# A two-part kernel (local and pooled attention, then a spatially gated MLP): mask and pooled v on TensorE for the first six head pairs, one buffer stock, and another table of durations for the planner

## The chip, the core and the metric

The kernel runs on one core of a Trainium2 chip. The metric is the device time of one execution in microseconds (us). The core has five engines with queues of their own, each worked off strictly in order: TensorE (PE in the profile, PEld for its weight loads), VectorE (DVE), ScalarE (ACT), GpSimdE (POOL) and SyncE (SP), which here only issues DMAs. The engines wait for each other by semaphores.

## The reference

Inputs are q, k, v of shape (8 batches, 8 heads, 576 positions, 64), all float32. For each head there are two attentions, and their sum is the head's output:

```python
q_d, k_d, v_d = means of q, k, v over groups of 4 positions      # 144 positions
out_up    = repeat(softmax(q_d k_d^T / 8) v_d, 4)                # pooled attention
out_local = softmax(where(|i - j| < 4, q k^T / 8, -1e9)) v       # a band of 7 keys per row
x = heads side by side of (out_up + out_local)                   # (8, 576, 512)

h = gelu_tanh(x @ w_in)                    # w_in 512 x 1024
u, v = two halves of h
v_n = (v - mean) / sqrt(var + 1e-6) * g_ln
v_s = w_sg @ v_n + b_sg                    # w_sg 576 x 576, over positions
out = x + (u * v_s) @ w_out                # w_out 512 x 512
```

## The kernel before, in words

The work of a batch has two parts. **Attention** goes by pairs of heads, four pairs (128 partitions: two heads of 64) per batch, 32 in all, numbered g. **The MLP** follows per batch and needs all four pairs of its batch.

Local attention is done in 10 blocks of 58 queries against 64 keys. For a pair the steps are (names of the tasks in the code in brackets): loads of q, k, and v in two layouts (lq, lk, lv, lw); sums of four neighbours of q, k and v (qs, ks, vs), the q sums spread by DMA into a block-diagonal tile (qx); the score product (S, line L403, 40 rows on TensorE); the mask of 0 and -1e30 added by VectorE while it copies the scores from PSUM to the tile ms, in two halves (ma, mb, L410); row maxima (mx, L424) and their product with minus the scale, the bias of the exponential (L426); exponentials with row sums on ScalarE (ea, eb, L436); reciprocals (rc); normalisation (np, L454). Pooled attention has the same steps on a smaller tile: Y (L420), my (L430, L431), ec (L444), nq (L457). The weights are then transposed by TensorE (T, U, t: L462, L467 and L469, L475), copied from PSUM (pa, pb, pc, pe), and multiplied with v: d (L500, pooled) and D (L520, local). VectorE adds both (xa, xb, L527), and x is split into a high and a low part (xh, xl, xc), so that three products of the faster float type give a float32 product.

The MLP has the products v (5 parts, L601), u, s and o (8 parts each, L680), with gelu, layer norm (vb, vp, vn: L632, L643, L651), splits (vh, vl, gh, gl: L198, L671, L735), bias and gate (sa, sm) and the final addition and store (oa, os) between. The last split ahead of the o product is gl (L735). At the start the weights are read as pairs of 32-bit words of a 64-bit format and turned into high and low parts: 24 pieces (eight each named y, z and r) through wb (L266, L268), wu, wq, wf (L282), wt (L287), wh (L198), wl (L293); w_sg needs whq and wlq alone.

The order is set by a planner that runs when the kernel is built. Every step is a `Task` with the engines that can do it and a duration on each, the tasks it comes after, the buffers it takes and gives back, and perhaps a due time. `plan` walks through a time of its own, gives a free engine the ready task with the least latest start, and so fixes, for each engine, the order in which its instructions are written. The chip then keeps that order and nothing else of the plan. `SIZES` and `CAPS` say how many buffers there are and how many of them a kind may hold: `ps` are the eight PSUM banks, `X`, `R` and `x` tiles in SBUF.

## Time and profile before

| | |
|---|---|
| runs | 664.25, 664.43, 661.49 us; median 664.25 us |
| the profiled execution | 664.12 us, of which the span from first to last instruction is 662.3 us |
| mean granted TensorE clock | 0.951 |
| busy: PE, PEld, DVE, ACT, POOL | 91%, 82%, 76%, 52%, 38% of the span |
| instructions | 16062 |
| chain that ended last | PE 72%, DVE 20%, issue 2%, POOL 2%, ACT 2%, DMA 1% |
| DMA | 60.29 MB, 91 GB/s on average |

How to read it: a busy share is a mean over the whole span, and the stages differ. The windows view gives busy time by stretch, the timeline the single instructions with the idle time before them and who ended it, the groups the mean duration by line and shape. PE rows are pipelined and their ends are modelled, so neighbouring rows overlap. An fp32 matmul shows as two rows.

### The profile page before, as it was taken

The numbers are of one execution on the slowest core, as the hardware profiler recorded it, in microseconds if no ns is written. First come the engines' busy times: TensorE is split into PE (matmuls) and PEld (weight loads), VectorE is DVE, ScalarE is ACT, GpSimd is POOL, SyncE is SP. The second block draws the span as 40 slices with busy tenths as digits, with TensorE's granted clock in tenths as the row PEclk, the third lists the DMA queues.
The fourth block names the chain that finished last, engine by engine and source line by source line (L and its number), as shares of the span: only waits on it lengthen the run. The fifth ranks groups of instructions, "written<-read, shape, count | busy, mean of one in ns | idle before, by whom it ended". The sixth has DMA issues, their size and how long they took to land.

```text
span 662.3 us, 16062 instructions
## 1 busy us (share of the span) xinstructions
PE 602.1 (91%) x6240; PEld 545.2 (82%) x6240; DVE 502.8 (76%) x1017; ACT 347.0 (52%) x1226; POOL 253.3 (38%) x298
## 2 busy tenths in 40 slices
PE   3767783989999999999999999999999999989997
PEld 3656572988899988989799888988898978979997
DVE  4899999999867949794888849794879759644452
ACT  3775776854757436654664446463664446350300
POOL 3476355474223424242434333342434233211210
PEclk9976766998999999999999999999999999989999
DMA  7666423423222330334222331224133430001001
GB/s 212 213 179 183 123 87 105 121 79 114 92 81 79 116 111 14 94 94 132 63 80 81 115 112 51 75 77 137 57 82 82 130 98 21 2 19 54 1 1 72
DMA packets 72684, 60.29 MB, mean 91 GB/s; under 512 B 17312, under 2 KB 56480, under 8 KB 72608
## 3 DMA queue, kind: packets, MB, share of 16 engines
q1 hardware_dynamic: 72608, 59.27, 29.8%
q8 instruction: 49, 0.80, 0.5%
q14 instruction: 27, 0.22, 0.1%
HBM read 47.45 MB, written 9.44 MB: 86 GB/s over the span
## 4 chain that ended last, share of the span: by engine, by line
PE 72%; DVE 20%; issue 2%; POOL 2%; ACT 2%; DMA 1%; SPq 0%; DVEq 0%; POOLq 0%; ACTq 0%
PE ps L680 43%; PE ps L601 14%; PE ps L520 3%; PE ps L403 3%; PE ps L500 3%; PE ps L420 3%; DVE ms L454 2%; PE ps L462 2%; DVE R L268 2%; DVE R L282 1%; DVE R L735 1%; ACT ms L436 1%; DVE stats L424 1%; DVE vs L716 1%; DVE ms L410 1%
## 5 line engine op out<-in xcount | busy, mean ns | idle before, releaser
L680 PE MATMUL ps<-wsg_h,R 128*128 128x288 f32 x576 | 123.0, 300 | 0.0
L680 PE MATMUL ps<-R,wout_h 128*128 128x288 f32 x512 | 111.3, 303 | 2.0 <-ACT wout_h L198 1.2
L436 ACT ACTIVATE ms<-ms,nb 128x64 f32<-128x64 f32 x320 | 106.8, 337 | 8.8 <-DVE nb L426 8.5
L680 PEld LDWEIGHTS ps<-wsg_h,R 128*128 128x128 f32 x576 | 93.7, 189 | 2.2 <-issue 1.2
L680 PE MATMUL ps<-wsg_l,R 128*128 128x288 f32 x320 | 92.5, 295 | 0.0
L680 PEld LDWEIGHTS ps<-R,wout_h 128*128 128x128 f32 x512 | 85.0, 191 | 4.3 <-ACT wout_h L198 1.4
L680 PE MATMUL ps<-X,win_h 128*128 128x288 f32 x256 | 80.3, 314 | 5.4 <-ACT R L697 2.9
L680 PE MATMUL ps<-R,win_h 128*128 128x288 f32 x256 | 77.8, 304 | 0.0
L680 PE MATMUL ps<-X,win_l 128*128 128x288 f32 x256 | 77.6, 303 | 0.0
L680 PE MATMUL ps<-R,wout_l 128*128 128x288 f32 x256 | 76.2, 298 | 0.3 <-DVE wout_l L293 0.3
L457 POOL TENSOR_TENSOR pd<-pd,rc 96x432 f32<-96x432 f32 x30 | 38.9, 1297 | 94.3 <-DVE rc L451 92.9
L601 PE MATMUL ps<-win_h,X 128*128 128x512 f32 x160 | 66.9, 418 | 1.4 <-ACT win_h L198 1.4
L601 PE MATMUL ps<-win_l,X 128*128 128x512 f32 x160 | 64.6, 404 | 3.8 <-DVE win_l L293 3.8
L751 DVE TENSOR_TENSOR x<-ps,x 128x288 f32<-128x288 f32 x64 | 29.0, 453 | 42.3 <-PE ps L680 42.3
L436 ACT ACTIVATION_READ_ACCUMULATOR ms<-ms,nb 128x1 f32 x320 | 60.7, 190 | 0.0
L680 PEld LDWEIGHTS ps<-wsg_l,R 128*128 128x128 f32 x320 | 60.3, 188 | 0.0
L680 PEld LDWEIGHTS ps<-X,win_h 128*128 128x128 f32 x256 | 50.4, 197 | 7.4 <-ACT R L697 3.3
L716 DVE SCALAR_TENSOR_TENSOR vs<-ps,g_sb,b_sb 128x288 f32<-128x288 f32 x64 | 32.8, 513 | 28.9 <-PE ps L680 28.7
L436 ACT ACT_TABLE_LOAD x22 | 28.2, 1283 | 48.6 <-DVE nb L426 48.4
L601 PE MATMUL ps<-win_h,R 128*128 128x512 f32 x128 | 51.4, 402 | 0.0
L680 PEld LDWEIGHTS ps<-R,win_h 128*128 128x128 f32 x256 | 50.5, 197 | 0.3
L680 PEld LDWEIGHTS ps<-X,win_l 128*128 128x128 f32 x256 | 50.4, 197 | 0.0
(103 smaller groups left out, 1385.9 us busy)
## 6 DMA issues: line engine op xcount, KB each, us to landing
vw<-in_vp_dram SPq DMA_DIRECT2D x64, 160.0 KB
q<-in_qT_dram SPq DMA_DIRECT2D x32, 293.0 KB
k<-in_kT_dram SPq DMA_DIRECT2D x32, 293.0 KB
v<-in_vp_dram SPq DMA_DIRECT2D x64, 144.0 KB
out_dram<-x SPq DMA_DIRECT2D x32, 288.0 KB
R<-in_w_in_dram SPq DMA_DIRECT2D x16, 256.0 KB
qd_bd<-qd SPq DMA_DIRECT2D x64, 36.0 KB
R<-in_w_out_dram SPq DMA_DIRECT2D x8, 256.0 KB
```

Source lines behind the costliest of these rows:

```text
L268: nc.vector.scalar_tensor_tensor(out=bits.bitcast(I32), in0=hw.bitcast(I32), scalar=-0x40000000, in1=bits.bitcast(I32), op0=ALU.bitwise_an ...
L403: nc.tensor.matmul(out=sp[i][os, c * KB:(c + 1) * KB], lhsT=q[hs, t * QB:t * QB + KB], rhs=k[hs, t * QB:t * QB + KB], start=True, stop=True)
L420: nc.tensor.matmul(out=st["sdv"][:, i, :], lhsT=qd_bd[par][:, i, :], rhs=st["kd"], start=True, stop=True)
L436: nc.scalar.activation(out=st["ms"][:, t, :], in_=st["ms"][:, t, :], func=AF.Exp, bias=st["nb"][:, t:t + 1], scale=scale, accum_out=sums[p ...
L454: ENG[e].tensor_tensor(out=st["ms"], in0=st["ms"], in1=bc_last(st["rc"][:, 0:NT], KB), op=ALU.mult)
L457: ENG[e].tensor_tensor(out=st["pd"], in0=st["pd"], in1=bc_last(st["rc"][0:96, NT:], SD), op=ALU.mult)
L500: nc.tensor.matmul(out=dn[hs].rearrange("p (i m) -> p i m", i=3), lhsT=vd[:, kt, hs], rhs=pdt[:, kt, :, h * 48:(h + 1) * 48], start=(kt == ...
L520: nc.tensor.matmul(out=at["ps", "o", g, i][hs, c * QB:(c + 1) * QB], lhsT=vw[ks, c, hs], rhs=pt[ks, c, h ^ i], start=True, stop=True)
L601: nc.tensor.matmul(out=acc, lhsT=r32(l), rhs=r32(w[:, k, DM:DF]), start=(i == 0), stop=(i == len(ops) - 1))
L680: nc.tensor.matmul(out=acc[:, 0:HALF], lhsT=r32(l), rhs=r32(r), start=(n == 0), stop=(n == len(ops) - 1))
L716: nc.vector.scalar_tensor_tensor(out=vsb[i], in0=at["ps", "m", b, "s", i][:, 0:HALF], scalar=g_sb[:, i // 2:i // 2 + 1], in1=b_sb[:, half( ...
L751: nc.vector.tensor_tensor(out=x[:, half(i)], in0=at["ps", "m", b, "o", i][:, 0:HALF], in1=x[:, half(i)], op=ALU.add)
```

## The change

For the first six pairs (`early`, g below 6: the four of batch 0 and two of batch 1):

- The mask is added on TensorE. Each of the two PSUM tiles of scores first gets a product of the identity with the mask (128 x 320), and the score products accumulate onto it. VectorE's two mask additions are gone; the row maxima read PSUM in two halves, and the exponentials read PSUM and write ms.
- The pooled product takes its four rows of v one by one: 16 small matmuls instead of 4, and GpSimdE's sum of v (vs, L391 and L392) is gone.

For all pairs the bias is a task of its own (nx, ny), which ScalarE or VectorE can do by a one-input multiplication. The loads of the first two pairs may be issued from ScalarE's queue. Attention tiles (q, k, the layouts of v, ms, pd, pt, pdt, x) come from the same stock of buffers as the MLP's, now 10 and 40; four PSUM banks instead of two may hold scores, two instead of one pooled scores. The planner has other durations, lengthens a VectorE task when GpSimdE works beside it and a TensorE task after idle time, holds loads back by a time given, and has other due times. So the order is another one throughout.

```diff
+COLD = 0.8
+AHEAD = 25.0
+SHARED = dict(np=0.6, nq=0.6, xl=0.6, wb=0.8, wf=0.6, wt=0.6, wl=0.6, wh=1.0, vn=0.3, vh=1.0, vl=0.6,
+              xh=1.0, sm=0.6, gh=1.0, gl=0.6, nx=0.3, ny=0.3)
+LONE = ("vp", "xc")
...
-    ready = [0.0] * n
+    ready = [max(t.hold, latest[i] - AHEAD) if t.mb else t.hold for i, t in enumerate(tasks)]
...
         end = now + t.engines[e]
+        if e == "V" and t.kind in SHARED:
+            end += SHARED[t.kind] * max(0.0, min(end, beside) - now)
+        if e == "P" and t.kind not in LONE:
+            beside = end
+        if e == "T":
+            idle = 0.85 * idle + 0.15 * min(1.0, (now - engine_at[e]) / 2.0)
+            end += COLD * min(1.0, 3.0 * idle) * t.engines[e]
...
-PERIOD, BASE, LEAD, MSBUFS = 67.0, 44.0, 12.0, 2
-SIZES = {"ps": 8, "X": 6, "R": 21, "x": 8}
-WIDTH = {"ps": 512, "X": XW, "R": S, "x": QB * NT}
-CAPS = {("ps", "s"): 2, ("ps", "d"): 1, ("ps", "t"): 3, ("ps", "o"): 2, ("ps", "m"): 4, ("R", "w"): 8, ("R", "v"): 3}
+PERIOD, BASE, LEAD, EARLY = 70.0, 40.7, 12.4, 6
+W_DUE = dict(y=40.0, z=53.0, r=84.0)
+HOLD = 0.0
+W_HOLD = dict(y=0.0, z=0.0, r=62.0)
+SIZES = {"ps": 8, "X": 10, "R": 40}
+WIDTH = {"ps": 512, "X": XW, "R": QPAD}
+CAPS = {("ps", "s"): 4, ("ps", "d"): 2, ("ps", "t"): 3, ("ps", "o"): 3, ("ps", "m"): 4, ("R", "w"): 12, ("R", "v"): 3,
+        ("R", "q"): 4, ("R", "k"): 4, ("X", "ms"): 4, ("X", "vw"): 4, ("R", "v4"): 8, ("R", "x"): 8}
...
         def scores(e):
             sp = [buf("ps", "s", g, i) for i in range(2)]
+            if early:
+                for i in range(2):
+                    nc.tensor.matmul(out=sp[i][:, 0:NTP * KB], lhsT=ident_sb, rhs=mask_sb[:, i:i + NTP, :],
+                                     start=True, stop=False, skip_group_check=True)
...
-                                         rhs=k[hs, t * QB:t * QB + KB], start=True, stop=True)
+                                         rhs=k[hs, t * QB:t * QB + KB], start=not early, stop=True,
+                                         skip_group_check=early)
...
         def top(e):
-            nc.vector.tensor_reduce(out=stats[par][:, 0:NT], in_=st["ms"], axis=AX.X, op=ALU.max)
-            st["nb"] = att.tile([P, NT + 3], F32, name="nb")
-            nc.vector.tensor_tensor(out=st["nb"][:, 0:NT], in0=stats[par][:, 0:NT], in1=nscale[:, 0:NT], op=ALU.mult)
+            if early:
+                for i in range(2):
+                    nc.vector.tensor_reduce(out=stats[par][:, i * NTP:(i + 1) * NTP], in_=spv(i), axis=AX.X, op=ALU.max)
+            else:
+                nc.vector.tensor_reduce(out=stats[par][:, 0:NT], in_=st["ms"].rearrange("p (c i) k -> p i c k", i=2),
+                                        axis=AX.X, op=ALU.max)
+
+        def bias(e):
+            st["nb"] = att.tile([P, NT], F32, name="nb")
+            if e == "A":
+                nc.scalar.mul(out=st["nb"], in_=stats[par][:, 0:NT], mul=-scale)
+            else:
+                nc.vector.tensor_scalar(out=st["nb"], in0=stats[par][:, 0:NT], scalar1=-scale, scalar2=None, op0=ALU.mult)
...
         def av_d(e):
-            for kt in range(2):
+            parts = [(kt, f) for kt in range(2) for f in range(FAC if early else 1)]
+            for n, (kt, f) in enumerate(parts):
                 for h in range(2):
...
+                                     lhsT=st["v4"][kt][:, f, hs] if early else st["vd"][:, kt, hs],
...
-        add(N("np"), {"P": 1.4, "V": 0.7}, norm, [N("rc")])
-        add(N("nq"), {"P": 0.96, "V": 0.5}, norm_d, [N("rc")])
+        add(N("np"), {"P": 1.42, "V": 0.78}, norm, [N("rc")])
+        add(N("nq"), {"P": 0.98, "V": 0.5}, norm_d, [N("rc")])
```

The order changes at every place; three of them follow. In these rows a line is one instruction or several equal ones (x), as out<-in with the program's names and the shape written. The first is the head of VectorE's queue, the first pair's steps. Before:

```order
L367 TENSOR_REDUCE qd<-q 128x144
L367 TENSOR_REDUCE kd<-k 128x144
L410 TENSOR_TENSOR ms<-ps_118,mask_sb 128x5x64
L410 TENSOR_TENSOR ms<-ps_119,mask_sb 128x5x64
L424 TENSOR_REDUCE stats_85<-ms 128x10
L426 TENSOR_TENSOR nb<-stats_85,nscale 128x10
```

And now, where lines have moved (L386 is L367 of before, L453 is L424, L463 the bias on VectorE), and where R_100 to R_108 are q and k of the first two pairs:

```order
L386 TENSOR_REDUCE qd<-R_100 128x144
L386 TENSOR_REDUCE kd<-R_102 128x144
L386 TENSOR_REDUCE qd<-R_105 128x144
L386 TENSOR_REDUCE kd<-R_108 128x144
L453 TENSOR_REDUCE stats_85<-ps_140 128x5
L453 TENSOR_REDUCE stats_85<-ps_141 128x5
L463 TENSOR_SCALAR nb<-stats_85 128x10
```

The second pair's sums have come ahead, and the mask additions are gone. The second place is TensorE's queue in batch 3 at the first transposes of that batch's time, those of the second pair of batch 4. Before, they stand after the second part of the u product:

```order
L680 MATMUL ps_4416<-R_4118,win_h 128x288
L680 MATMUL ps_4416<-X_4116,win_l 128x288
L475 MATMUL ps_4439<-ident_sb,pd 72x96 x3
L462 MATMUL ps_4445<-ident_sb,ms 128x128 x4
L467 MATMUL ps_4451<-ident_sb,ms 128x128
L469 MATMUL ps_4451<-ident_sb,pd 72x96 x3
```

Now they stand after its fourth part and after the third pair's score product (L426 now), with the pooled weights (L522, L475 before) last:

```order
L426 MATMUL ps_4567<-R_4065,R_4054 64x64 x2
L426 MATMUL ps_4566<-R_4065,R_4054 64x64 x2
L426 MATMUL ps_4567<-R_4065,R_4054 64x64 x2
L509 MATMUL ps_4600<-ident_sb,X_4440 128x128 x4
L514 MATMUL ps_4608<-ident_sb,X_4440 128x128
L516 MATMUL ps_4608<-ident_sb,R_4197 72x96 x3
L522 MATMUL ps_4616<-ident_sb,R_4197 72x96 x3
```

The transposes have moved back by two parts of u and one score product. The third place is VectorE's queue at the end of batch 3's s product, with the steps sa (L716) for the seventh and eighth part, and the reciprocals and normalisation (L450, L451, L454) of the last pair of batch 4. Before:

```order
L716 SCALAR_TENSOR_TENSOR vs<-ps_4899,g_sb,b_sb 128x288
L198 CAST R_4943<-R_4584 128x576
L735 TENSOR_TENSOR R_4950<-R_4584,R_4943 128x576
L716 SCALAR_TENSOR_TENSOR vs<-ps_4926,g_sb,b_sb 128x288
L450 TENSOR_SCALAR rc<-sums_88 128x13
L451 RECIPROCAL rc<-rc 128x13
L723 TENSOR_TENSOR R_4687<-R_4687,vs 128x288
L454 TENSOR_TENSOR ms<-ms,rc 128x640
```

And now (L777 is sa, L784 the gate, L501 the normalisation):

```order
L777 SCALAR_TENSOR_TENSOR vs<-ps_4983,g_sb,b_sb 128x288
L497 TENSOR_SCALAR rc<-sums_88 128x13
L498 RECIPROCAL rc<-rc 128x13
L784 TENSOR_TENSOR R_4650<-R_4650,vs 128x288
L501 TENSOR_TENSOR X_4826<-X_4826,rc 128x640
L777 SCALAR_TENSOR_TENSOR vs<-ps_5013,g_sb,b_sb 128x288
L784 TENSOR_TENSOR R_4809<-R_4809,vs 128x288
L777 SCALAR_TENSOR_TENSOR vs<-ps_5039,g_sb,b_sb 128x288
```

The reciprocals and the normalisation have moved ahead of the bias steps of the last two parts of s.

More of the change, by code (lines that the diff above doesn't have):

```diff
@@ L97, in plan @@
     func_on, where, given, out = {}, {}, [], []
-    dma_at = now = 0.0
-    ready = [0.0] * n
+    dma_at = now = beside = 0.0
+    idle = 1.0
+    ready = [max(t.hold, latest[i] - AHEAD) if t.mb else t.hold for i, t in enumerate(tasks)]
     pending = {i for i in range(n) if not left[i]}
@@ L431, in top_d @@
-            nc.vector.tensor_tensor(out=st["nbd"][0:96], in0=stats[par][0:96, NT:], in1=nscale[0:96, NT:], op=ALU.mult)
-        def exp(half):
-            def emit(e):
-                for t in range(half * 5, half * 5 + 5):
-                    nc.scalar.activation(out=st["ms"][:, t, :], in_=st["ms"][:, t, :], func=AF.Exp,
-                                         bias=st["nb"][:, t:t + 1], scale=scale,
+            if e == "A":
+                nc.scalar.mul(out=st["nbd"][0:96], in_=stats[par][0:96, NT:], mul=-scale_d)
+            else:
+                nc.vector.tensor_scalar(out=st["nbd"][0:96], in0=stats[par][0:96, NT:], scalar1=-scale_d,
+                                        scalar2=None, op0=ALU.mult)
@@ new lines, in exp @@
+        def exp(i):
+            def emit(e):
+                if early and i == 0:
+                    st["ms"] = buf("X", "ms", g).rearrange("p (t k) -> p t k", k=KB)
+                for c in range(NTP):
+                    t = 2 * c + i
+                    src = spv(i)[:, c] if early else st["ms"][:, t, :]
+                    nc.scalar.activation(out=st["ms"][:, t, :], in_=src, func=AF.Exp,
+                                         bias=st["nb"][:, i * NTP + c:i * NTP + c + 1], scale=scale,
@@ L575, in attention @@
[L575 to L578 removed]
+        hold = HOLD + (g - NPAIR) * 3.0 if g >= NPAIR else 0.0
@@ new lines, in attention @@
+        ahead = 4 if early else 2
+        dq = {"S": 0.8, "A": 0.9} if g < 2 else {"S": 0.8}
+        dq2 = {"S": 1.4, "A": 1.6} if g < 2 else {"S": 1.4}
+        add(N("lq"), dq, load_q, [N("S", ahead), N("qs", ahead)], takes=[("R", "q", g)], mb=0.3, hold=hold)
+        add(N("lk"), dq, load_k, [N("S", ahead), N("ks", ahead)], takes=[("R", "k", g)], mb=0.3, hold=hold)
+        add(N("lv"), dq2, load_v4, [N("d", ahead // 2)], takes=[("R", "v4", g, 0), ("R", "v4", g, 1)], mb=0.3)
+        add(N("lw"), dq2, load_vw, [N("D", ahead)], takes=[("X", "vw", g)], mb=0.33)
@@ new lines, in attention @@
+        add(N("qs"), {"V": 0.68, "P": 1.3}, qsum, [N("lq"), N("qx", 2)], gives=[("R", "q", g)])
+        add(N("qx"), {"S": 1.3}, qspread, [N("qs"), N("Y", 2)], mb=0.07)
+        add(N("ks"), {"V": 0.68, "P": 1.3}, ksum, [N("lk"), N("Y", 2)], gives=[("R", "k", g)])
+        if not early:
+            add(N("vs"), {"P": 2.25}, vsum, [N("lv"), N("d", 2)], gives=[("R", "v4", g, 0), ("R", "v4", g, 1)])
+        add(N("S"), {"T": 1.8 if early else 0.74}, scores, [N("lq"), N("lk"), N("D", ahead)] + (["ident", "mask"] if early else []), takes=[("ps", "s", g, 0), ("ps", "s", g, 1)], gives=[("R", "q", g), ("R", "k", g)])
@@ new lines, in attention @@
+        if not early:
+            add(N("ma"), {"V": 0.4}, masked(0), [N("S"), "mask"], takes=[("X", "ms", g)], gives=[("ps", "s", g, 0)])
+            add(N("mb"), {"V": 0.4}, masked(1), [N("S"), N("ma")], gives=[("ps", "s", g, 1)])
+        add(N("Y"), {"T": 0.74}, scores_d, [N("qx"), N("ks")], takes=[("ps", "d", g)])
+        add(N("mx"), {"V": 1.0 if early else 0.82}, top, ([N("S")] if early else [N("ma"), N("mb")]) + [N("nx", 2)])
+        add(N("nx"), {"A": 0.25, "V": 0.16}, bias, [N("mx"), N("ea", 2), N("eb", 2)])
@@ L784, in mlp @@
             end = i == 2 * KT - 1
-            add(N("u", i), {"T": 1.6}, u_mm(i), xn + w + ([N("v", s) for s in range(NS)] if end else []),
+            add(N("u", i), {"T": 1.62}, u_mm(i), xn + w + ([N("v", s) for s in range(NS)] if end else []),
                 takes=[("ps", "m", b, "u", i)], due=end_at,
```

153 lines of the change are left out of this document (75 added, 78 removed).

## The prediction, on record before the run

> **What bounds the kernel now.** First the page's engine shares.
>
> ```profile
> PE   602.1 (91%) x6240; PEld 545.2 (82%) x6240; DVE 502.8 (76%) x1017; ACT 347.0 (52%) x1226; POOL 253.3 (38%) x298
> ```
>
> The mean over the span says TensorE. It hides two regimes, so second comes the windows view, cut where stages end. Columns: stretch; length; busy us (instructions) of PE, weight loads, DVE, ACT, POOL; granted TensorE clock; DMA share; GB/s.
>
> ```profile
> 0.00:52.00 52.00, 30.86 (x476) 25.13 (x480) 41.26 (x88) 31.11 (x152) 27.49 (x44) 0.86 0.67 200
> 52.00:72.00 20.00, 12.64 (x155) 9.43 (x155) 19.64 (x40) 8.97 (x27) 12.90 (x16) 0.67 0.74 208
> 72.00:90.00 18.00, 15.07 (x100) 12.25 (x101) 17.62 (x42) 16.01 (x51) 6.90 (x8) 0.88 0.15 43
> 90.00:127.00 37.00, 26.25 (x226) 24.12 (x225) 33.95 (x63) 26.23 (x78) 20.18 (x23) 0.70 0.37 113
> 127.00:151.00 24.00, 21.69 (x256) 20.40 (x257) 22.75 (x41) 14.91 (x51) 16.29 (x18) 0.90 0.34 98
> 151.00:237.40 86.40, 84.96 (x842) 78.52 (x841) 68.31 (x143) 47.14 (x159) 28.78 (x33) 0.99 0.30 92
> 237.40:604.00 366.60, 356.79 (x3838) 324.61 (x3837) 272.84 (x550) 194.71 (x696) 131.54 (x148) 1.00 0.26 79
> 604.00:662.30 58.30, 53.85 (x361) 50.73 (x359) 26.48 (x57) 7.96 (x16) 9.21 (x10) 1.00 0.07 26
> ```
>
> Up to 151 us VectorE works 135.2 us (the first five rows) and TensorE 106.5 us, at a clock between 0.67 and 0.90. From 151 on TensorE is busy 98% and VectorE 79% or less. The seam is where batch 0's output product starts. The timeline there, then the first matmuls of batch 2 and of batch 7:
>
> ```profile
> 148.88 1.95 DVE L735 TENSOR_TENSOR R<-R,R 128x576 fp32r<-128x576 f32 x2
> 151.31 0.61 PE L680 MATMUL ps<-R,wout_h 128*128 128x288 f32 x1
> 237.38 0.51 PE L601 MATMUL ps<-win_h,X 128*128 128x512 f32 x1
> 603.91 0.39 PE L601 MATMUL ps<-win_h,X 128*128 128x512 f32 x1
> ```
>
> L735 is the last VectorE step that this product needs; it ends at 150.8 and TensorE follows 0.5 us later. So VectorE's queue sets the end of the first stage. Batches 2 to 6 then take (603.91 - 237.38)/5 = 73.3 us each. Third, the timeline of batch 3 for what TensorE waits for; brackets hold its idle time and the releaser.
>
> ```profile
> 317.68 0.74 PE ps L403 x40
> 322.15 4.67 PE ps L601 x20
> 328.64 2.07 POOL L457 TENSOR_TENSOR pd<-pd,rc 96x432 f32<-96x432 f32 x1 [4.83 <-DVE rc L451]
> 329.13 0.81 DVE L454 TENSOR_TENSOR ms<-ms,rc 128x640 f32<-128x640 f32 x1
> 330.76 0.44 PE L475 MATMUL ps<-ident_sb,pd 96*72 96x96 f32 x3 [0.76 <-POOL pd L457]
> ...
> 364.86 0.98 PE L420 MATMUL ps<-kd,qd_bd 128*96 128x144 f32 x6
> 365.53 0.93 POOL L457 TENSOR_TENSOR pd<-pd,rc 96x432 f32<-96x432 f32 x1 [1.55 <-DVE rc L451]
> 366.51 0.44 PE L475 MATMUL ps<-ident_sb,pd 96*72 96x96 f32 x3 [0.68 <-POOL pd L457]
> 367.19 0.66 PE L462 MATMUL ps<-ident_sb,ms 128*128 128x128 f32 x4 [0.24 <-DVE ms L454]
> ```
>
> (The first two rows, a pair's score product and the last two parts of the batch's first product, are the chain view's.) A batch has two stalls, both at transposes of attention weights that are not normalised yet.
>
> **The change part by part, first stage.** I count VectorE instructions up to that last subtraction of batch 0, in the order before (264) and after (238), and price them with the VectorE groups of the window 0 to 151 (count, busy us, mean ns):
>
> ```profile
> L410 DVE TENSOR_TENSOR ms<-ps,mask_sb 128x320 f32<-128x320 f32 x18 | 8.4, 474 | 3.0 <-PE ps L403 2.4 <-PE ps L467 0.6
> L424 DVE TENSOR_REDUCE stats<-ms 128x10 f32<-128x640 f32 x9 | 7.2, 802 | 0.1
> L426 DVE TENSOR_TENSOR nb<-stats,nscale 128x10 f32<-128x10 f32 x9 | 3.5, 392 | 0.3
> L431 DVE TENSOR_TENSOR nbd<-stats,nscale 96x3 f32<-96x3 f32 x9 | 3.0, 334 | 0.3
> L430 DVE TENSOR_REDUCE stats<-ps 96x3 f32<-96x432 f32 x9 | 5.4, 595 | 1.3 <-PE ps L420 1.3
> L454 DVE TENSOR_TENSOR ms<-ms,rc 128x640 f32<-128x640 f32 x7 | 9.3, 1334 | 0.0
> L198 DVE COPY pdt<-ps 72x288 f32<-72x288 f32 x11 | 4.8, 443 | 0.0
> L268 DVE SCALAR_TENSOR_TENSOR R<-R,R 128x256 int32<-128x256 int32 x20 | 12.5, 627 | 0.7
> L266 DVE TENSOR_SCALAR R<-R 128x256 int32<-128x256 int32 x20 | 8.3, 417 | 0.0
> L282 DVE SCALAR_TENSOR_TENSOR R<-R,R 128x256 f32<-128x256 f32 x20 | 12.6, 659 | 0.1
> ```
>
> - Mask additions, 18 to 5: -13 x 0.474 = -6.2.
> - Row maxima: 9 x 0.802 = 7.2 become 12 half ones read from PSUM and 2 whole ones. A half is not in the trace; the nearest row, L430, reads PSUM too, and 320/432 of 0.595 is 0.44. 12 x 0.44 + 2 x 0.80 = 6.9: -0.3. Bounds 0.40 (half of L424) to 0.60 (L430 whole): -0.8 to +1.6.
> - Bias products: 9 x 0.392 + 9 x 0.334 = 6.5 go to ScalarE, six remain on VectorE as one-input operations. Bounds: 0.17 each (half an L431) and 0.39 (L426); I take 0.25: -5.0.
> - Maxima of the pooled scores, 9 to 8: -0.6. Normalisations, 7 to 5: -2.7. Copies of transposed weights, 18 to 9, priced by pdt for the seven that are of that kind and nothing for the two short ones: -3.1.
> - Weight splitting comes earlier: all 24 pieces now stand ahead of this point, 20 before: +4 x (0.627 + 0.417 + 0.659) = +6.8.
> - Eleven further kinds (sums of q and k, splits, casts), net six fewer, at the stage's mean of 135.2/264 = 0.51: -3.1.
>
> Sum: -14.2. VectorE's 15.8 idle us in the stage I leave as they are. What is added elsewhere: **TensorE** gets per early pair two mask products (2 x 320 columns) and 12 more small pooled products. Rows of the chain of batch 3 give the rates (x counts rows; an fp32 matmul has two), and two groups what GpSimdE loses (means over the whole run):
>
> ```profile
> L391 POOL TENSOR_TENSOR vd<-v 72x512 f32<-72x512 f32 x32 | 44.9, 1404 | 6.1 <-DMA v<-in_vp_dram 6.1
> L392 POOL TENSOR_TENSOR vd<-vd 72x256 f32<-72x256 f32 x32 | 27.9, 872 | 54.4 <-PE ps L500 53.5
> 335.22 0.64 PE ps L500 x8
> 336.61 1.79 PE ps L680 x12
> 339.13 0.91 PE ps L420 x6
> ```
>
> Six L420 rows (864 columns) take 0.91 us, so a pair's mask (four rows, 1280 columns) takes 1.3; eight L500 rows take 0.64, so 24 more take 1.9. Six pairs: 19 us at full clock, 38 at half. 106.5 + 19 = 126 stays under the 137 below, and one pair less stands ahead of the seam: cost zero, covered by TensorE's idle time; without that cover it is the 38. **ScalarE** gets about ten biases and ten copies (10 us on 97.2 of 151): covered. Six of the first pairs' loads (nine DMAs) move from SP's queue to ScalarE's; they stand ahead of its first exponential, which can't start before the first maxima, and SP's queue is shorter by them: zero. In the early pairs the scores stay in PSUM until the exponentials have read them; what queues behind that is the next score product on TensorE, and with four banks instead of two it is the product after the next one, under VectorE's queue like the rest: zero. The pooled product now waits for the load of v alone, no longer for GpSimdE. **GpSimdE** loses 6 x (1.404 + 0.872) = 13.7 us and takes q/k sums and weight steps instead. The common buffer stock only lets loads be asked for earlier; the DMA engines are 0.67 to 0.74 busy up to 72 us, so there is room, and I take no cost. Without that room batch 0's first product waits for its weights, under the same VectorE queue. So the output product starts at 151.3 - 14.2 = 137.1.
>
> From there to batch 2 TensorE is the bound, 86.1 us before. The new order puts one attention pair's products more into this stretch (score product 0.74, pooled scores 0.91, transposes 0.66 + 0.44, the last product, which has forty rows too, 0.74: 3.5 us). Batch 2 starts at 137.1 + 86.1 + 3.5 = 226.7 instead of 237.4: **-10.7**.
>
> **Steady state.** The brackets give 0.76 + 0.68 + 0.24 = 1.7 us per batch, the window 237.4 to 604 gives (366.60 - 356.79)/5 = 2.0, some of it unexplained. In the new order the first transposes stand two products and one score product later, and the second normalisation stands ahead of two bias steps of VectorE that wait for products, with the transposes straight behind the last gate product. Between a score product (the 317.68 row) and its normalised weights (the L454 row's end) lie 329.94 - 317.68 = 12.3 us; the new order puts 0.74 + 4.67 + 4 x 1.79 + 0.74 = 13.3 us of TensorE work between its start and the transposes. Both stalls should go, the first with 1.0 us to spare. I take the 2.0, five times (9.81 in all): **-9.8**. The last batch has no attention beside it and keeps its 58.3.
>
> **Sum.** Span 662.3 - 10.7 - 9.8 = 641.8. The profiled execution took 664.12, 1.8 more than its span and 0.1 under the median of 664.25: 641.8 + 1.8 = **643.6 us**, 3.1% faster.
>
> **Rivals.** (A) *VectorE gains more, because GpSimdE lets go of it.* Rows for it: L454 takes 0.81 at 329.13 and 1.33 on average at the start, and
>
> ```profile
> 104.06 2.79 POOL L287 TENSOR_TENSOR R<-R,R 128x256 int32<-128x256 int32 x4
> 104.12 5.05 DVE L651 TENSOR_SCALAR R<-R,mv,rs 64x512 f32<-64x512 f32 x1 [0.44 <-POOL rs L643]
> 106.81 2.08 POOL L293 TENSOR_TENSOR win_l<-R,win_h 128x256 fp32r<-128x256 f32 x3
> ```
>
> one VectorE instruction ends only when seven GpSimdE ones that follow each other are done. With 13.7 us less of GpSimdE, 5 x 0.5 for the five L454 left and 4.2 of this one (it has fewer elements per row than an L454 of 0.81) could come back: 643.6 - 6.7 = 637; if the extra pair's 3.5 us also find idle time of TensorE, 633. The Trainium skill (SBUF — State Buffer, Who interferes with whom) calls the shared port pair an exclusive lock, held for a whole instruction, and lets whoever issues first block the other fully; the 5.05 row agrees. By that rule alone the sum would be case A's.
>
> (B) *The same lock, other way round.* The new order strings GpSimdE work together too: five splits of w_sg in a row, then two sums of two instructions each and a pooled v of four, then five steps on w_out. Three blocks like the 5.05 row cost 3 x 4.2 = 12.6: 656. (C) *The stalls only move.* If a batch still costs 73.3, 643.6 + 9.8 = 653. The early TensorE work at half clock (106.5 + 38 = 144.5 instead of 137.1) gives 651; both belong here.
>
> (D) *Slower: TensorE waits for the first transposes of each batch.* The bias now is a ScalarE step that queues behind the fourth gelu of the batch, and the reserve is 1.0 us. Each us beyond it costs five. It decides from 4.8 us on: 643.6 + 5 x 4.8 = 668. Against it: a bias is short, and the ScalarE is 47% idle there. (E) *Nothing*: gains and new waits cancel, 664.
>
> **Chances.** Forecast (638 to 650) 0.58, A 0.12, B 0.09, C 0.09, D 0.07, E 0.05. Faster by over 0.5% 0.88, within 0.5% (what a measurement here can tell from no change) 0.05, slower 0.07. The range goes from A's lower end with a few us for the bounds of the maxima and biases (627) to B (656, and one for its own rounding); it leaves out D and E.
>
> **What the new profile would show.** Batch 0's output product starts near 137, VectorE about 120 us busy up to there; batch 2 starts near 227; batches 2 to 6 take 71.3 each with no idle time ahead of the transposes; TensorE's share rises above 94% although 168 more matmul rows run. The forecast is wrong if VectorE is idle for more than 20 us before 137, if its two-input groups run longer than in the rows above, or if TensorE waits at the first transposes of a batch.

## The result, and the profile after the change

The changed kernel takes 646.49 us (median of 4 runs, 645.77 to 647.49); the kernel before took 664.07 in the same job (661.49 to 664.43). The ratio is 0.9744 with a 95% interval of 0.9716 to 0.9773: 2.6% faster, where 643.6 us and 3.1% were forecast. The profiled execution took 645.77 us, 1.9 more than its span. First the engine shares on the page of the changed kernel.

```profile
span 643.9 us, 16520 instructions
PE 605.0 (94%) x6408; PEld 547.7 (85%) x6408; DVE 479.0 (74%) x956; ACT 352.4 (55%) x1279; POOL 252.4 (39%) x347
```

The windows view of the changed kernel is cut at four marks: the first matmul of batch 0's first product (64.5), of its output product (138.5), of batch 2 (227.5) and of batch 7 (585.2). Columns as in the prediction: stretch; length; busy us (instructions) of PE, weight loads, DVE, ACT, POOL; granted clock; DMA share; GB/s.

```profile
0.00:64.50 64.50, 45.74 (x681) 36.86 (x681) 45.73 (x95) 39.06 (x187) 26.75 (x44) 0.89 0.78 208
64.50:138.50 74.00, 62.80 (x597) 55.14 (x596) 70.86 (x144) 52.80 (x164) 50.47 (x59) 0.90 0.35 105
138.50:227.50 89.00, 88.29 (x938) 81.50 (x936) 64.22 (x128) 51.72 (x196) 35.29 (x51) 0.99 0.32 91
227.50:585.20 357.70, 353.87 (x3840) 323.07 (x3839) 270.45 (x531) 200.71 (x719) 133.96 (x188) 1.00 0.28 82
585.20:643.90 58.70, 54.34 (x362) 51.13 (x360) 27.77 (x60) 8.07 (x16) 5.89 (x7) 0.99 0.07 26
```

The same first two stretches of the kernel before:

```profile
0.00:61.90 61.90, 38.52 (x617) 31.74 (x618) 50.90 (x109) 35.92 (x168) 34.48 (x52) 0.83 0.66 194
61.90:151.30 89.40, 68.30 (x592) 59.89 (x591) 84.62 (x161) 61.30 (x188) 49.28 (x55) 0.79 0.38 111
```

So the first stage has two halves, and the prediction treated it as one. Up to the first product nothing was gained (61.9 to 64.5 us), and VectorE is idle for 18.8 of the 64.5 us. From there to the output product 15.4 us went, and VectorE is busy 70.86 of 74.00. The span's 18.4 us are then: 12.8 up to the output product, less 2.9 on the way to batch 2 (89.0 us instead of 86.1), 8.8 in batches 2 to 6 (357.7 instead of 366.5), less 0.3 in the last batch.

The timeline of the changed kernel at the seam: TensorE comes to the output product (L741) straight from transposes (L509) that had waited for VectorE (L501).

```profile
135.82 1.45 DVE L501 TENSOR_TENSOR X<-X,rc 128x640 f32<-128x640 f32 x1
...
137.33 0.80 PE L509 MATMUL ps<-ident_sb,X 128*128 128x128 f32 x4 [0.24 <-DVE X L501]
...
138.53 0.59 PE L741 MATMUL ps<-R,wout_h 128*128 128x288 f32 x1
```

In batches 2 to 6 one stall of two is left. What TensorE waits for there (in total, times, and the longest), first in the kernel before, then in the changed kernel:

```profile
PE ps L475 <- POOL pd L457: 7.1, 8, 2.0
PE ps L475 <- DVE mv L633: 1.6, 2, 0.8
PE ps L462 <- DVE ms L454: 1.2, 5, 0.2
```

```profile
PE ps L509 <- DVE X L501: 3.4, 5, 0.7
PE ps L548 <- ACT R L220: 0.5, 1, 0.5
```

And the timeline of the changed kernel at that place in batch 3:

```profile
320.35 0.91 POOL L504 TENSOR_TENSOR R<-R,rc 96x432 f32<-96x432 f32 x1 [2.24 <-DVE rc L498]
320.40 2.78 DVE L501 TENSOR_TENSOR X<-X,rc 128x640 f32<-128x640 f32 x1
321.22 1.28 POOL L732 TENSOR_TENSOR R<-R,R 128x512 fp32r<-128x512 f32 x1
...
323.32 0.63 PE L509 MATMUL ps<-ident_sb,X 128*128 128x128 f32 x4 [0.67 <-DVE X L501]
```

VectorE's normalisation (L501) starts 0.05 us behind a GpSimdE instruction (L504) and ends at 323.18, which is 0.68 us after the end of the next GpSimdE instruction (L732, 322.50). In the prediction's row of batch 3 it had taken 0.81.

### The profile page after: what moved, and what is told of

Same layout as the page of the kernel before. It is cut to its first block, busy times and chain, and to the rows that moved or that the text cites. A ratio compares the mean times of both kernels' runs of the same rounds, so it can differ in the third digit from the quotient of the medians.

```text
span 643.9 us, 16520 instructions
## 1 busy us (share of the span) xinstructions
PE 605.0 (94%) x6408; PEld 547.7 (85%) x6408; DVE 479.0 (74%) x956; ACT 352.4 (55%) x1279; POOL 252.4 (39%) x347
## 4 chain that ended last, share of the span: by engine, by line
PE 71%; DVE 13%; ACT 5%; DMA 4%; POOL 3%; issue 2%; SPq 1%; ACTq 0%; POOLq 0%; DVEq 0%
PE ps L741 42%; PE ps L662 12%; PE ps L569 4%; PE ps L548 3%; PE ps L444 3%; ACT X L483 3%; DVE X L501 2%; PE ps L426 2%; PE ps L509 2%; DVE R L301 2%; DMA R<-in_kT_dram 1%; DMA R<-in_vp_dram 1%; PE ps L522 1%; POOL wsg_l L344 1%; PE ps L516 1%
## 5 line engine op out<-in xcount | busy, mean ns | idle before, releaser
L741 PE MATMUL ps<-wsg_h,R 128*128 128x288 f32 x576 | 125.7, 305 | 2.2 <-DVE R L732 2.2
L741 PE MATMUL ps<-R,wout_h 128*128 128x288 f32 x512 | 109.3, 302 | 0.7 <-DVE R L220 0.5
L741 PEld LDWEIGHTS ps<-wsg_h,R 128*128 128x128 f32 x576 | 95.6, 192 | 4.6 <-DVE R L732 2.7
L741 PE MATMUL ps<-wsg_l,R 128*128 128x288 f32 x320 | 93.8, 299 | 0.0
L483 ACT ACTIVATE X<-X,nb 128x64 f32<-128x64 f32 x260 | 86.8, 335 | 1.8 <-DVE nb L463 1.4
L741 PEld LDWEIGHTS ps<-R,wout_h 128*128 128x128 f32 x512 | 84.4, 190 | 3.0 <-issue 1.4
L741 PE MATMUL ps<-X,win_h 128*128 128x288 f32 x256 | 77.7, 304 | 0.5 <-ACT R L758 0.5
L220 ACT COPY R<-ps 72x288 f32<-72x288 f32 (+3 forms) x116 | 38.4, 397 | 71.0 <-PE ps L509 52.3
L741 PE MATMUL ps<-R,wout_l 128*128 128x288 f32 x256 | 76.1, 297 | 0.0
L741 PE MATMUL ps<-X,win_l 128*128 128x288 f32 x256 | 75.7, 296 | 0.0
L741 PE MATMUL ps<-R,win_h 128*128 128x288 f32 x256 | 75.6, 295 | 0.0
L704 POOL TENSOR_TENSOR rs<-rs,nhalf 128x1 f32<-128x1 f32 (+1 forms) x40 | 25.0, 627 | 108.8 <-DVE rs L695 105.5
L662 PE MATMUL ps<-win_h,X 128*128 128x512 f32 x160 | 66.9, 418 | 0.0
L812 DVE TENSOR_TENSOR R<-ps,R 128x288 f32<-128x288 f32 x64 | 29.2, 457 | 47.2 <-PE ps L741 46.4
L741 PEld LDWEIGHTS ps<-wsg_l,R 128*128 128x128 f32 x320 | 61.5, 192 | 0.0
L674 ACT ACTIVATE R<-ps 128x512 f32<-128x512 f32 x32 | 19.2, 599 | 68.4 <-PE ps L662 55.3
L741 PEld LDWEIGHTS ps<-X,win_h 128*128 128x128 f32 x256 | 48.2, 188 | 2.6 <-issue 1.2
L410 POOL TENSOR_TENSOR vd<-R 72x256 f32<-72x256 f32 x52 | 41.6, 799 | 21.9 <-DMA R<-in_vp_dram 12.0
L741 PEld LDWEIGHTS ps<-R,wout_l 128*128 128x128 f32 x256 | 48.8, 191 | 0.0
L483 ACT ACTIVATION_READ_ACCUMULATOR X<-X,nb 128x1 f32 x260 | 48.7, 187 | 0.0
```

The costliest lines, as they stand in the source:

```text
L220: (nc.scalar.copy if e == "A" else ENG[e].tensor_copy)(**kw)
L410: ENG[e].tensor_tensor(out=vd2, in0=v[:, 0:2], in1=v[:, 2:4], op=ALU.add)
L483: nc.scalar.activation(out=st["ms"][:, t, :], in_=src, func=AF.Exp, bias=st["nb"][:, i * NTP + c:i * NTP + c + 1], scale=scale, accum_out= ...
L662: nc.tensor.matmul(out=acc, lhsT=r32(l), rhs=r32(w[:, k, DM:DF]), start=(i == 0), stop=(i == len(ops) - 1))
L674: nc.scalar.activation(out=v, in_=acc, func=AF.Gelu_apprx_tanh)
L704: nc.gpsimd.tensor_tensor(out=rs[0:n], in0=rs[0:n], in1=nhalf[0:n], op=ALU.pow)
```

## The experiments

All marks are start times of TensorE's first matmul of that product in the profiled execution; medians and ratios are from the timed runs, each against the kernel before on the same chip. The runs were made on several chips; differences below are of medians, and the ratios give values up to 1 us away from them (for pool_sums 7.1 us instead of 7.7). The marks are those of one execution, which in no_early was the fastest of four (651.83) and in mask_only the slowest (655.03).

| kernel | first product | output product | batch 2 | batch 7 | median us | ratio (95%) |
|---|---|---|---|---|---|---|
| before | 61.9 | 151.3 | 237.4 | 603.9 | 664.07 | 1 |
| changed | 64.5 | 138.5 | 227.5 | 585.2 | 646.49 | 0.9744 (0.9716 to 0.9773) |
| vec_mask_time | 63.8 | 138.2 | 226.8 | 584.6 | 646.29 | 0.9752 (0.9726 to 0.9778) |
| vec_late | 64.7 | 144.4 | 233.1 | 590.8 | 651.09 | 0.9799 (0.9785 to 0.9813) |
| pe_mask_twice | 67.1 | 141.3 | 230.0 | 587.7 | 647.16 | 0.9743 (0.9729 to 0.9757) |
| v_loads_later | 63.6 | 137.9 | 226.7 | 584.4 | 644.46 | 0.9703 (0.9688 to 0.9718) |
| pool_sums | 69.0 | 147.6 | 236.3 | 594.0 | 654.19 | 0.9851 (0.9834 to 0.9868) |
| vl3_on_vec | 63.9 | 138.2 | 227.0 | 581.2 | 642.08 | 0.9667 (0.9649 to 0.9684) |
| both_fixes | 64.5 | 138.7 | 227.4 | 581.5 | 640.42 | 0.9642 (0.9624 to 0.9660) |
| mask_only | 66.9 | 149.3 | 237.3 | 594.8 | 652.61 | 0.9830 (0.9808 to 0.9851) |
| pooled_only | 63.3 | 140.8 | 227.8 | 585.5 | 646.76 | 0.9737 (0.9722 to 0.9751) |
| no_early | 74.1 | 146.6 | 233.9 | 591.6 | 654.60 | 0.9861 (0.9840 to 0.9882) |
| no_rules | 65.7 | 143.8 | 230.3 | 584.1 | 645.53 | 0.9720 (0.9697 to 0.9743) |
| old_caps | 79.0 | 146.0 | 235.0 | 596.6 | 656.46 | 0.9888 (0.9870 to 0.9906) |

The kernels down to both_fixes keep the changed kernel's order but for the edit; the last five are planned anew, so that their order differs in many places.

### Is the first stage bound by VectorE's queue?

**vec_mask_time**: the mask's additions are put back on VectorE, without use.

```diff
         def top(e):
             if early:
+                for i in range(2):
+                    nc.vector.tensor_tensor(out=<part of wsg_l that is filled later>, in0=spv(i), in1=mask_sb[:, i:i + NTP, :], op=ALU.add)
                 for i in range(2):
                     nc.vector.tensor_reduce(...)
```

> The changed kernel with its order kept, and in each of the first six pairs two additions of the mask on VectorE again, ahead of the maxima, whose results nothing reads: 12 instructions of 128x320 at about 0.47 us, 5.7 us more on VectorE up to the start of batch 0's first output product. Theory of the prediction (VectorE's queue sets the first stage): that start moves from 138.5 us to 143 to 145 and the time from 646.5 to 651 to 653. Rival (VectorE's 21.9 us of idle time there take it in): the start stays within 138 to 140 and the time within 646 to 648.

The median did not change (646.29, although two of the five runs took 649.1 and 649.6), nor did the start of the output product (138.2): the rival holds. VectorE's groups up to there (count, busy us, mean ns), first in the changed kernel, then with the additions, which are L453 there:

```profile
L301 DVE SCALAR_TENSOR_TENSOR R<-R,R 128x256 f32<-128x256 f32 x24 | 15.9, 685 | 0.0
...
L285 DVE TENSOR_SCALAR R<-R 128x256 int32<-128x256 int32 x24 | 9.7, 406 | 0.0
L306 DVE CUSTOM_DVE_ANT_0 R<-R,R 128x512 uint16<-128x512 uint16 x11 | 8.5, 787 | 0.0
```

```profile
L301 DVE SCALAR_TENSOR_TENSOR R<-R,R 128x256 f32<-128x256 f32 x24 | 14.2, 616 | 0.0
...
L285 DVE TENSOR_SCALAR R<-R 128x256 int32<-128x256 int32 x24 | 8.5, 354 | 0.0
L306 DVE CUSTOM_DVE_ANT_0 R<-R,R 128x512 uint16<-128x512 uint16 x11 | 6.7, 620 | 0.0
...
L453 DVE TENSOR_TENSOR wsg_l<-ps,mask_sb 128x320 fp32r<-128x320 f32 x12 | 5.2, 474 | 4.6 <-PE ps L426 4.6
```

Twelve additions of 0.474 us came, and three unchanged groups became 4.7 us shorter. GpSimdE did the same work in both. So part of what the profile calls busy on VectorE is time in which an instruction is held up, and extra work ahead of it took the place of that time. Single instructions show it: an L285 of the changed kernel with no GpSimdE instruction beside it takes 0.28 us, and the one at 63.87, under GpSimdE instructions all through, 1.33.

**vec_late**: 6.5 us more on VectorE behind the first product.

```diff
         def shift(e):
-            nc.vector.tensor_scalar(out=bits..., in0=hw..., ...)
+            for _ in range(2 if t[0] in "zr" else 1):
+                nc.vector.tensor_scalar(out=bits..., in0=hw..., ...)
```

> The changed kernel with its order kept; in the splitting of the weights marked z and r the first VectorE instruction of line 285 runs twice with the same result: 16 instructions of 0.41 us, 6.5 us more on VectorE, and all of them between 64 and 125 us, where VectorE is busy 70.9 of 74 us. (Additions of 5.7 us on VectorE ahead of 64 us had cost nothing.) Theory of the prediction, held to this stretch (from the first v product at 64.5 us to the first output product at 138.5 VectorE's queue sets the pace): the output product moves to 143 to 145 us and the time from 646.5 to 651 to 653. Rival (the first stage is set all through by transfers and TensorE, and VectorE's queue has room): 646 to 648.

The output product moved to 144.4 (+5.9) and the time by 4.6 us. The windows view from the first product to the output product of this kernel:

```profile
64.70:144.40 79.70, 62.46 (x598) 54.57 (x596) 77.12 (x160) 52.84 (x164) 50.08 (x60) 0.89 0.32 100
```

VectorE is busy 77.12 instead of 70.86 us, and the stretch is 5.7 us longer. So VectorE's queue does set the pace behind 64 us; ahead of it the 5.7 us that were tried cost nothing.

**pe_mask_twice**: the mask's product runs twice on TensorE.

```diff
-                for i in range(2):
-                    nc.tensor.matmul(out=sp[i]..., lhsT=ident_sb, rhs=mask_sb[:, i:i + NTP, :], start=True, ...)
+                for i in range(4):
+                    nc.tensor.matmul(out=sp[i % 2]..., lhsT=ident_sb, rhs=mask_sb[:, i % 2:i % 2 + NTP, :], start=(i < 2), ...)
```

> The changed kernel with its order kept; in the first six pairs the product that adds the mask runs twice on TensorE (the masked places then hold twice the large negative number, the probabilities are the same): 24 more matmuls, 1.3 us per pair at the full clock and 2.4 us at half, so 8 to 14 us more on TensorE, all ahead of 56 us. Theory of the prediction (TensorE's added work in the first pairs lies beside other work): the first v product stays within 64 to 66 us and the time within 645.5 to 648. Rival (ahead of 64 us the chain of transfers and TensorE at a low clock now sets the pace, VectorE having room there): the first v product moves by 6 to 12 us and the time to 652 to 658.

The first product came 2.6 us later, more than the theory allowed; the median stayed (647.16, ratio 0.9743). The mask's added work on TensorE is covered in good part. That of the pooled product was not varied.

**v_loads_later**: the trace showed a new early wait, on two small transfers of the changed kernel:

```profile
7.29 2.47 PE L419 MATMUL ps<-mask_sb,ident_sb 128*128 128x320 f32 x4 [7.29 <-DMA ident_sb<-in_ident_dram]
...
16.61 0.95 PE L444 MATMUL ps<-kd,qd_bd 128*96 128x144 f32 x6 [3.36 <-DMA qd_bd<-qd]
```

In the changed kernel three of the four loads of v are on ScalarE's queue, the fourth is on SyncE's already.

```diff
+    late = {"qx0": ("lv0", "lw0"), "qx1": ("lv1", "lw1")}     # in the order: issued by SyncE, right behind these
```

> The changed kernel with its order kept, but the four loads of v of pairs 0 and 1 are issued by SyncE, right behind the small transfers of the pooled q of those pairs, and no longer by ScalarE in the first microseconds. Theory (the early transfers crowd each other: the identity and the small transfer of pooled q land late because the loads of v start beside them): the first mask product starts before 6 us instead of at 7.29, VectorE's idle time up to the start of batch 0's first output product falls from 21.9 us to 16 to 19, and the time from 646.5 us to 640.5 to 643.5. Rival 1 (the early bytes arrive as fast as the queues carry them, whatever the order): a load that goes later only moves the wait to the pooled product of pairs 0 and 1, and the time stays within 645 to 648. Rival 2 (SyncE's queue is the narrow place): its loads behind the four come later and the time goes up by 1 to 3 us, to 648 to 650.

The pooled score products of the first pairs in this kernel:

```profile
12.38 0.98 PE L444 MATMUL ps<-kd,qd_bd 128*96 128x144 f32 x6
...
17.52 1.73 PE L444 MATMUL ps<-kd,qd_bd 128*96 128x144 f32 x6 [2.34 <-DMA qd_bd<-qd]
...
28.74 1.72 PE L444 MATMUL ps<-kd,qd_bd 128*96 128x144 f32 x6 [3.03 <-DMA qd_bd<-qd]
```

That of pair 0 starts at 12.38 instead of 16.61 and no longer waits for its transfer, but the next two now wait 5.4 us (1.04 and 0.61 in the changed kernel). The first mask product starts at 6.75 (the theory said before 6), the first product came only 0.9 us and the output product 0.6 us earlier. The median fell by 2.0, less than the theory's 3 to 6; the intervals of the ratios still touch. Early transfers do crowd each other, and most of the wait moves to the next pairs. What sets the first 64 us was not isolated beyond this.

### What is GpSimdE's time worth?

**pool_sums**: the sums of v return to GpSimdE, without use.

```diff
         def av_d(e):
+            if early:
+                vsum("P")
             od = buf("ps", "o", g, 0)
```

> The changed kernel with its order kept; in the first six pairs GpSimdE makes the sums of v again (four instructions, about 2.3 us of work per pair, 13.7 us in all) just ahead of the pooled product, which still reads v itself: nothing reads the sums. (Replanned with the sums in use, the kernel took 652.6.) Theory (the pooled part's gain is GpSimdE's time: what is queued behind the sums on GpSimdE comes later, and VectorE instructions beside them are held up): 650 to 655. Rival (GpSimdE has room, and the loss of the replanned kernel lay in its order, where VectorE took over work that GpSimdE had no place for): 646 to 648.

654.19, 7.7 us above the changed kernel, with TensorE's and VectorE's own instructions as they were. The timeline of this kernel (its lines behind the edit are two higher) shows how:

```profile
96.53 0.53 POOL L411 TENSOR_TENSOR vd<-vd 72x128 f32<-72x128 f32 x1
96.66 5.07 DVE L734 TENSOR_TENSOR R<-R,R 128x512 fp32r<-128x512 f32 x1
97.03 4.15 POOL L344 TENSOR_TENSOR wsg_l<-R,wsg_h 128x576 fp32r<-128x576 f32 x3
...
104.52 0.40 PE L743 MATMUL ps<-X,win_h 128*128 128x288 f32 x1 [3.47 <-DVE R L578]
```

A subtraction that has 0.68 us of work on VectorE took 5.07, until a last part of a sum of v and three splits of w_sg behind it had ended on GpSimdE, and TensorE waited 3.47 us for what stood behind it in VectorE's queue. The groups up to the output product:

```profile
L285 DVE TENSOR_SCALAR R<-R 128x256 int32<-128x256 int32 x24 | 14.2, 590 | 0.0
...
L734 DVE TENSOR_TENSOR R<-R,R 128x512 fp32r<-128x512 f32 x4 | 7.3, 1835 | 0.0
```

L285 was 9.7 us above, and L734 is L732 in the changed kernel's groups:

```profile
L732 DVE TENSOR_TENSOR R<-R,R 128x512 fp32r<-128x512 f32 x4 | 3.2, 802 | 0.1
```

That is 4.5 + 4.1 = 8.6 us more for the same instructions; VectorE's busy time up to the output product rises by 7.8 in all (116.6 to 124.4). Half of the delay lies ahead of the first product (69.0 instead of 64.5). The longest L285 stands there, with GpSimdE's work beside it nearly all through:

```profile
52.65 4.10 DVE L285 TENSOR_SCALAR R<-R 128x256 int32<-128x256 int32 x1
```

So the sums cost their time on VectorE, by holding it up. How the 4.10 us reach the first product was not followed.

**vl3_on_vec**: one GpSimdE instruction of the string in the steady state goes to VectorE.

```diff
+    order = [(x[0], "V" if x[0].name in [f"vl{b}.3" for b in range(2, 7)] else x[1]) for x in order]
```

> The changed kernel with its order kept, but in batches 2 to 6 the subtraction that makes the low part of the fourth row block of v (line 732) runs on VectorE and not on GpSimdE. Theory (VectorE's normalisation of the probabilities, line 501, is held up because two GpSimdE instructions run one behind the other under it): that normalisation falls from 2.78 us to 1.2 to 1.9, the 0.67 us for which TensorE waits ahead of the transposes of line 509 goes in each of the five batches, and the time falls by about 3.4 us, from 646.5 to 642 to 644. Rival (VectorE's 0.7 us more per batch stand in the same queue ahead of the normalisation or of something else that TensorE waits for): 646 to 648.

642.08: 4.4 us less, and the theory holds. The same place in this kernel's timeline, then its steady window:

```profile
319.08 0.91 POOL L504 TENSOR_TENSOR R<-R,rc 96x432 f32<-96x432 f32 x1 [2.23 <-DVE rc L498]
319.12 1.54 DVE L501 TENSOR_TENSOR X<-X,rc 128x640 f32<-128x640 f32 x1
320.59 0.68 DVE L732 TENSOR_TENSOR R<-R,R 128x512 fp32r<-128x512 f32 x1
...
321.32 0.66 PE L509 MATMUL ps<-ident_sb,X 128*128 128x128 f32 x4
```

```profile
227.00:581.20 354.20, 353.73 (x3841) 323.17 (x3840) 266.06 (x536) 200.53 (x719) 128.11 (x183) 1.00 0.28 83
```

L501 takes 1.54 instead of 2.78, the transposes wait for nothing, TensorE is busy 353.73 of 354.20 us, and a batch takes 70.8 us. VectorE's extra subtraction (0.68) costs nothing there. Of the 4.4 us the trace shows 3.6 in batches 2 to 6 (357.7 to 354.2).

**both_fixes** has the edits of v_loads_later and vl3_on_vec.

> The two edits together: the four loads of v of pairs 0 and 1 issued by SyncE behind the small transfers of pooled q, and the subtraction of line 732 for the fourth row block on VectorE in batches 2 to 6. If both theories hold the gains add, since one lies ahead of 140 us and the other behind 227 us: 637 to 640.5 us. If only one holds, that one's own time; if neither, 645 to 650.

640.42, the fastest kernel here, 3.6% under the kernel before. The medians agree with two gains that add (2.0 + 4.4 = 6.4 expected, 6.1 measured), but the interval of the ratio overlaps with that of vl3_on_vec, and the profiled execution, like that of v_loads_later alone, shows no gain in the first stage beyond the spread of the marks. That the first edit still gains beside the second is not shown.

### Which part of the change brings what?

**pooled_only** and **mask_only** split the early pairs' two edits; both are planned anew. In pooled_only one of an early pair's two banks of scores is still given back only by the exponentials, other than before the change.

```diff
+        added = False       # pooled_only: in the lines on the mask, its maxima and exponentials
+        direct = False      # mask_only: in the lines on the sums of v and the pooled product
```

> The changed kernel replanned, with the pooled product of the first six pairs straight from v, but the mask added by VectorE there as before the change (12 more instructions of 0.48 us on VectorE, 24 matmuls less on TensorE). Theory of the prediction (each microsecond that VectorE loses ahead of the first output product comes off the time): 651 to 654. Rival (VectorE work ahead of 64 us lies in its idle time, and TensorE is what counts there): 640 to 647.

> The changed kernel replanned, with the mask still added by TensorE in the first six pairs but the pooled product fed from the sums of v made on GpSimdE, as before the change. If the mask's leaving VectorE makes the gain of the first stage: 645 to 649. If the pooled part is worth something by itself (six sums of 2.2 us leave GpSimdE, four more matmul groups per pair come to TensorE): 649 to 653; if its TensorE work is on the path: 640 to 645.

Without the mask's product the time is the same (646.76); without the pooled product straight from v it is 652.61, 6.1 us more. So the mask's part brings nothing that can be measured, and the pooled part most of what the early pairs bring.

**no_early** sets EARLY to 0.

```diff
-PERIOD, BASE, LEAD, EARLY = 70.0, 40.7, 12.4, 6
+PERIOD, BASE, LEAD, EARLY = 70.0, 40.7, 12.4, 0
```

> The changed kernel replanned with no early pairs: mask on VectorE and sums of v on GpSimdE in all pairs; buffers, caps and the planner's costs stay. If the two parts add as they did alone (the mask 0, the pooled product 6): 651 to 654. If either alone hides the other's worth: above 655. If the early pairs' work is worth nothing and the replanned kernel without the pooled part was an unlucky order: 645 to 649. What is left to the 664 of before is the share of the planner and the buffers.

654.60, between the two theories' ranges: 8.1 us, about what pool_sums alone costs. A batch still takes (591.6 - 233.9)/5 = 71.5 us: the early pairs' work has no part in the steady state's gain.

**no_rules** takes out the planner's two new costs.

```diff
-COLD = 0.8
+COLD = 0.0
...
-        if e == "V" and t.kind in SHARED:
+        if False and e == "V" and t.kind in SHARED:
```

> The changed kernel replanned without the two new costs of the planner (VectorE's time beside GpSimdE, TensorE's time after idle stretches); durations, buffers and the early pairs' work stay. If these costs are what makes the order good (the two waits at transposes in each batch, the first stage): 652 to 662, with TensorE waiting again ahead of transposes in batches 2 to 6. If the measured durations and the buffers do it: 644 to 650.

645.53, no worse. The first stage's order is worse without them (143.8 at the output product, 230.3 at batch 2) and the steady state's better: in batches 2 to 6 TensorE's only wait of this kernel is

```profile
PE ps L548 <- ACT R L220: 0.5, 1, 0.5
```

and a batch takes 70.8 us. The planner's price for work beside GpSimdE did not avoid the string of GpSimdE instructions at the transposes; the order planned without it has none there. In batch 3 of this kernel VectorE makes the subtraction L732 itself, and its normalisation starts just ahead of GpSimdE's:

```profile
322.70 0.82 DVE L501 TENSOR_TENSOR X<-X,rc 128x640 f32<-128x640 f32 x1
322.75 1.55 POOL L504 TENSOR_TENSOR R<-R,rc 96x432 f32<-96x432 f32 x1 [3.11 <-DVE rc L498]
```

In the changed kernel the same two start 0.05 us apart the other way round, and there L504 takes 0.91 and L501 2.78. Who starts first decides who is held up here.

**old_caps** has the limits of before on the banks of scores, pooled scores and outputs.

```diff
-CAPS = {("ps", "s"): 4, ("ps", "d"): 2, ("ps", "t"): 3, ("ps", "o"): 3, ...
+CAPS = {("ps", "s"): 2, ("ps", "d"): 1, ("ps", "t"): 3, ("ps", "o"): 2, ...
```

> The changed kernel replanned with the limits of before on banks for scores (2 and not 4), pooled scores (1 and not 2) and outputs (2 and not 3). The scores of early pairs then hold their two banks until the exponentials have read them, and TensorE's next score product waits for that. If the larger stock carries the gain: 652 to 664, most of it lost ahead of the first v product. If the prediction is right that the banks cost and bring nothing by themselves: 645 to 650.

656.46, 10.0 us more. The masked score products (L419 opens each) of the first three pairs in this kernel, and then those of the second and third in the changed kernel:

```profile
7.29 2.47 PE L419 MATMUL ps<-mask_sb,ident_sb 128*128 128x320 f32 x4 [7.29 <-DMA ident_sb<-in_ident_dram]
...
17.36 1.72 PE L444 MATMUL ps<-kd,qd_bd 128*96 128x144 f32 x6 [6.33 <-DMA qd_bd<-qd]
18.88 2.34 PE L419 MATMUL ps<-mask_sb,ident_sb 128*128 128x320 f32 x4
...
33.36 2.26 PE L419 MATMUL ps<-mask_sb,ident_sb 128*128 128x320 f32 x4
```

```profile
10.96 1.55 PE L419 MATMUL ps<-mask_sb,ident_sb 128*128 128x320 f32 x4
...
17.40 1.24 PE L419 MATMUL ps<-mask_sb,ident_sb 128*128 128x320 f32 x4
```

With two banks the second pair's scores come 7.9 us later and the third's 16.0; the first product starts at 79.0. The limit acts through the order: the wait that the trace shows ahead of the second pair's scores is not one for a bank but that of the pooled score product (L444) for its transfer, and this product now stands in front of them. The stretch behind it is shorter by 7.0, since more of VectorE's work was then done (61.24 us ahead of the first product, 45.73 in the changed kernel), and 7.5 us stay at the output product. A batch takes 72.3 us, 0.8 more than in the changed kernel: so about 3.9 of the 8.8 us of the steady state are missing in the order that the planner makes with the old limits.

## Why the prediction was right, and where not

The time came out 2.9 us above the forecast, and the marks were met: the output product at 138.5 (137.1 forecast), batch 2 at 227.5 (226.7), 71.5 us per batch (71.3), the last batch 58.7 (58.3). The steps behind them fared worse.

- **VectorE's work in the first stage, -14.2 with its idle time unchanged.** The windows give 135.5 us before and 116.6 after, -18.9, and an idle time of 21.9 instead of 15.8. Two errors of 5 and 6 us cancelled; that the mark of 137.1 was met is in part luck. Of the first error, 2.0 are the weight steps, which rose by 4.8 and not 6.8; and the step that had taken 5.05 us, which the prediction had left to rival A, now takes 0.54 (L712 now; other groups grew, so the parts come to more than the whole):

```profile
L712 DVE TENSOR_SCALAR R<-R,mv,rs 64x512 f32<-64x512 f32 x1 | 0.5, 539 | 1.7 <-POOL rs L704 1.7
```

The step that failed is the rule that each VectorE microsecond ahead of the seam comes off the time. vec_late shows it for the stretch behind 64 us; vec_mask_time shows that it does not hold ahead of it.
- **Mask additions, -6.2**: worth nothing (vec_mask_time, pooled_only). They were priced rightly, 0.474 each. The 12 of the early pairs stood ahead of 64 us, where VectorE had room.
- **A half maximum**, 0.44 taken: 12 of them took 0.472 each, within the bounds; the row of the changed kernel:

```profile
L453 DVE TENSOR_REDUCE stats<-ps 128x5 f32<-128x320 f32 x12 | 5.2, 472 | 3.8 <-PE ps L426 3.8
```

- **GpSimdE loses 13.7 us, at no gain by itself**: wrong; put back in the same order the sums cost 7.7 us (pool_sums). That is rival A's mechanism, which I priced at 6.7 and gave 0.12. VectorE's idle time grew by 6.1 us beside it, and the total stayed in the forecast's range.
- **Banks, zero**: wrong. old_caps loses 10.0 us. The prediction asked what the new order forbids and not what order the old limits would have given. The common buffer stock in SBUF was not varied alone, so its zero is open. The shares do not add up: pooled product and banks alone would make 17.7 of the 17.6 us, and neither can be called the cause of the whole.
- **TensorE's 19 us more in the early pairs, hidden**: right for the mask's part. Doubling it cost 0.7 us in the median, within the spread. The pooled part was not doubled.
- **Six load issues on ScalarE's queue, zero**: nearly. 2.0 us came back when the loads of v went later (v_loads_later), and the wait for qd_bd was not foreseen.
- **89.6 us from the seam to batch 2**: 89.0.
- **Both stalls of a batch go, -9.8**: -8.8. The second went. The first shrank to 0.67 us; what is left of it is no lack in the reserve of 1.0 us of TensorE's work: VectorE was held up behind two GpSimdE instructions, which is rival B's lock at a place that B did not name. Without it the batch takes 70.8 us (vl3_on_vec), so the step's size was a little low and the lock took 3.6 (trace) to 4.4 us (medians) back. The idle time of TensorE per batch fell from 2.0 to (357.70 - 353.87)/5 = 0.8 us; the rest of the 1.8 us is a busy time that is 0.6 shorter for nearly the same number of records. Most of that lies in one group of the output product's rows (R,wout_h, 320 rows in each kernel, 70.0 us before and 67.5 now); why is open.

One reading of the prediction was too even: it has TensorE 98% busy from 151 us on, which holds for the stretch to 237 alone; its rows give 97.3% in batches 2 to 6 and 92% in the last. Of the three signs named for a wrong forecast, two came (VectorE idle for more than 20 us before the seam, and a wait at the first transposes); of the third, longer two-input groups, only one (L301, 685 ns where L282 had 659). The time held all the same, since the sum had errors of both signs. What remains open is which of the durations, loads and buffers gave the rest of the steady state's gain (73.3 us a batch before, 72.3 with the old limits). The new costs of the planner are not needed for it, since no_rules has 70.8.

The Trainium skill (SBUF — State Buffer, Who interferes with whom) calls the port pair that VectorE and GpSimdE share an exclusive lock, and says of VectorE's two-port modes that whoever issues first holds it for the whole instruction while the other blocks fully; a VectorE instruction with two inputs in SBUF contends with a GpSimdE instruction that reads SBUF. The rows of L501 and L504 in the changed kernel and in no_rules agree with it. They and the prediction's 5.05 row show one thing more: the blocked VectorE instruction did not get in between two GpSimdE instructions that follow each other; 2.78 us ended only 0.68 after the second, and 5.07 us ended 0.55 after a row of four. The prediction's row at 328.64 shows something like it on the other side: GpSimdE's L457 starts 0.49 us ahead of VectorE's L454, but takes 2.07 where L454 takes 0.81; another VectorE instruction (L618, from 328.52 on) was running when it started. Whether that one held GpSimdE up was not tested.
